# Where the stores of attention rows are issued, and how the first expert slot's weights are spread over the steps

## The chip, the cores and the metric

The kernel runs on one core of a Trainium2 chip. The core has five engines that each run their own list of instructions in order: TensorE (PE in the profile; its weight loads are shown apart as PEld), VectorE (DVE), ScalarE (ACT), GpSimd (POOL) and SyncE (SP), which here computes nothing and mainly issues DMAs. ScalarE and GpSimd issue DMAs too; such an issue stands in the profile as ACTq, SPq or POOLq. Instructions of different engines wait for each other through semaphores.

The metric is the device time of one execution in microseconds, given as the median of several runs. "About 1%" below means what a measurement of this kernel can tell from no change.

## The reference

Two stages follow each other. The first is banded attention, 8 batches of 8 heads, 576 positions, 64 values a head; heads 0 to 3 see the last 32 positions, heads 4 to 7 every fourth of the last 128. The second takes the 4608 rows of 512 that come out, picks one of 8 experts for each by a gate, and runs that expert's two layers.

```python
def _attn_ref(q, k, v):                      # 8, 8, 576, 64
    window, dilation = 32, 4
    scores = scale * np.matmul(q, k.transpose(0, 1, 3, 2))
    rel = pos[:, None] - pos[None, :]
    mask_plain = (rel >= 0) & (rel < window)
    mask_dil = (rel >= 0) & (rel < window * dilation) & (rel % dilation == 0)
    ...
    return np.matmul(softmax(scores), v)
...
def _moe_ref(x, modality_id, w_gate, modality_bias, w1, w2):   # x 4608 x 512
    logits = x @ w_gate + modality_bias[modality_id]
    e_idx = np.argmax(logits, axis=1)
    ...
    for e in range(E):                       # w1[e] 512 x 1024, w2[e] 1024 x 512
        mask = e_idx == e
        h = np.maximum(x[mask] @ w1[e], 0.0)
        out[mask] = gate_w[mask, None] * (h @ w2[e])
```

## The kernel before

**Attention steps.** The queries of a batch are cut into 9 units (m = 0 to 8; m below 5 belongs to heads 0 to 3, the rest to heads 4 to 7), 72 units in all, and two units make one step. The main loop runs over the steps t; the code's `state['t']` counts units, so it is 2t. A step computes the scores of its own two units (tile pss), the exponential of the step before (sm), the transposed probabilities (ptt, pT) and the product with the values (po, vw), and for the units of two steps back it divides by the sum: VectorE writes x_sb (L399), a tile with three buffers, each of which holds the rows of two units.

**Stores and loads.** At the end of a step, `Unit.keep(queue)` stores the x_sb of units two steps back to x_dram, two arrays in main memory, one for each half of the heads. Units 1 and 3 of a batch store 256 KB in one DMA (L419), units 6 and 8 store 256 KB (L422), and unit 4 stores 64 KB (L412) and two pieces of 32 KB (L415). Here `keep` is called with ScalarE's queue (L1240), but the two pieces of L415 name SyncE themselves. All loads of attention are in SyncE's list: keys (`load_one`, L118 and L121, tile st), queries (the same lines), values (`load_v`, L141, tile vw), one to three steps ahead of use. Within a step the order is: queries, values, then at the end of the step keys.

**Experts.** The rows are routed into slots of 256 rows of one expert. Four slots hold rows of batches 0 to 2 alone and are made ready during the attention. For a slot, GpSimd gathers its rows by number from x_dram (L313, tile xr); SyncE writes them to x_slot in main memory (L807) and reads them back in another order as xg in four quarters (L813); VectorE transposes them (L958, tile xt, in two halves), ScalarE rounds them to xh (L964), and VectorE subtracts to get the rest, xl (L967). The weights come by `fetch_weights`: each half of w1 in four quarters of 256 KB (L828, tiles w1q), and w2 in four pieces of 512 KB (L831, tiles w2q); ScalarE and VectorE split them in high and low parts, and TensorE multiplies each pair of parts (L1028 for the first layer, L1008 for the second). The first expert matmuls run beside the last attention steps.

**What sets the order.** PE, VectorE, ScalarE and SyncE run in the order in which the program writes their instructions ("manual schedule"). GpSimd's order is set by the scheduler. Background work of the expert stage (routing, gathers, weights) is written as generators, which `advance()` steps at fixed places of each step, one `yield` at a time. `first_slot` (L887) is the one for slot 0: it calls `load_more(0, 1)`, which takes the next piece from `fetch_weights`, at units 48, 62, 64, 66, 67 and 68, and between them steps `prepare_x(0, ...)`, which holds the transposes and xl. One piece there is either 512 KB of w2 or a whole half of w1, that is four DMAs at once. `loads_of[n][1]` counts the pieces of slot n that are out, six being all; `hold` and `ahead` go by it later.

The DMAs that SyncE and ScalarE issue share eight semaphores, which the program gives out in turn.

Of the kernel before, what the change touches and what calls it, by code (L numbers as in the profile page):

```python
# [22 lines left out]
B, H, S, D = 8, 8, 576, 64  # L23
# [35 lines left out]
def kernel(  # L59
# [12 lines left out]
    nc = tc.nc  # L72
# [51 lines left out]
    def load_qk(b, kd, queue=nc.sync):  # L124
        kn = load_one(b, kd, k)
        return load_one(b, kd, q, queue), kn
# [24 lines left out]
    state = {('qk', 0, 0): load_qk(0, 0, nc.scalar)}  # L151
# [45 lines left out]
    KC, FC = DM // P, FF // P  # L197
# [168 lines left out]
    class Unit:  # L366
# [41 lines left out]
        def keep(self, queue):  # L408

            b, xs = self.b, self.xs  # L410
            if self.m == 4:
                queue.dma_start(out=x_dram[0][b * S + TQ * (NTILE - 1):(b + 1) * S, :], in_=xs[0:TQ, 0])  # L412
                rows = x_dram[1][b * S:(b + 1) * S, :].rearrange("(a p) c -> p a c", a=2)[TQ * HT:HP]
                for hp in range(2):
                    nc.sync.dma_start(out=rows[:, :, 2 * D * hp:2 * D * (hp + 1)],  # L415
                                    in_=xs[TQ + HR * hp:TQ + HR * (hp + 1), 0].rearrange("p (a c) -> p a c", a=2))
            elif self.m in (1, 3):
                r0 = b * S + 2 * TQ * (self.m - 1)
                queue.dma_start(out=x_dram[0][r0:r0 + 2 * P, :].rearrange("(u p) c -> p u c", p=P), in_=xs)  # L419
            elif self.m in (6, 8):  # L420
                rows = x_dram[1][b * S:(b + 1) * S, :].rearrange("(a p) c -> p a c", a=2)
                queue.dma_start(out=rows[P * self.ip:P * (self.ip + 1)], in_=xs)  # L422
# [394 lines left out]
    def fetch_weights(si, first):  # L817

        e = nc.sync.value_load(si[0:1, 0:1], min_val=0, max_val=NE - 1)
        kw = {}  # L820
        if not first:
            kw = dict(cond=nc.sync.value_load(si[0:1, 2:3], min_val=0, max_val=1), cond_hint=False)
        w1v = w1[ds(e, 1)].rearrange("o (r m p) f -> (o r) p m f", r=KC, p=BLK)

        def half(i):
            cols = slice(HALFF * P * i, HALFF * P * (i + 1))
            for r in range(KC):
                nc.sync.dma_start(out=w1q[i][BLK * r:BLK * (r + 1)], in_=w1v[r, :, :, cols], **kw)  # L828

        def pair(c):  # L830
            nc.sync.dma_start(out=w2q[c], in_=w2[ds(e, 1), 2 * P * c:2 * P * (c + 1), :].rearrange("o (a p) m -> p (o a) m", p=P), **kw)  # L831

        for piece, i in ((pair, 0), (half, 0), (pair, 1), (pair, 2), (half, 1), (pair, 3)):
            piece(i)
            yield


# [6 lines left out]
    ids_of, si_of, fetching, loads_of = {}, {}, [], {}  # L844
# [22 lines left out]
    def load_more(n, pieces):  # L867

        if n not in loads_of and n in si_of:
            loads_of[n] = [fetch_weights(si_of[n], n == 0), 0]  # L870
        if n in loads_of:
            for _ in range(min(pieces, 6 - loads_of[n][1])):
                next(loads_of[n][0], None)
                loads_of[n][1] += 1
# [12 lines left out]
    def first_slot():  # L887

        prep = prepare_x(0, ids_of[0])
        for n, at in enumerate((48, 62, 64, 66, 67, 68)):  # L890
            while state['t'] < at:
                if n > 2:
                    next(prep, None)
                yield
            load_more(0, 1)
            yield
        yield from prep

# [48 lines left out]
    def prepare_x(n, ids):  # L947


        nu = ids[1]  # L950
        while ('xg', n) not in state:
            yield
        xg = state['xg', n]
        xh = xpre.tile([P, KC, SLOT], F32R, name="xh")
        xl = xpre.tile([P, KC, SLOT], F32R, name="xl")
        for u in range(nu):
            xt = xpre.tile([P, KC, P], F32, name="xt", bufs=1)
            nc.vector.transpose(out=xt.rearrange("p m (g i) -> p g m i", i=BLK),  # L958
                                in_=xg[:, KC * u:KC * (u + 1)].rearrange("p g (m c) -> p g m c", c=BLK))
            if u == nu - 1:  # L960
                taken.add(n)
            yield
            ts = slice(P * u, P * (u + 1))
            nc.scalar.copy(out=xh[:, :, ts], in_=xt)  # L964
            if n == 0:
                yield
            nc.vector.tensor_tensor(out=xl[:, :, ts], in0=xt, in1=xh[:, :, ts].bitcast(F32), op=ALU.subtract)  # L967
            if u < nu - 1:
                yield
        state['x', n] = xh, xl  # L970
# [158 lines left out]
    pairs, queue, late = [], [], []  # L1129
# [26 lines left out]
    for t in range(NPAIR + 4):  # L1156
        state['t'] = 2 * t
        here = [divmod(i, 9) for i in (2 * t, 2 * t + 1)] if t < NPAIR else []
        for b, m in here:
            if m == 0:  # L1160
                state['lT', b] = gwk.tile([2 * LGP, S], F32, name="lT")
            units.append(Unit(b, m, [state['v', b, 0], state['v', b, 1]] if m >= 4 else [state['v', b, 0]], state['lT', b]))
        if here:
            pairs.append(Pair(units[-2:]))
            pairs[t].scores()
            if t < 2:
                keep_busy((4, 8)[t])
        if t == NPAIR - 1:
            sctx.close()
            psum['y'] = ctx.enter_context(tc.tile_pool(name="ps_y", bufs=2, space=PSUM))  # L1170
            assert 'go' in state
            moe = slots(NS, ids_of, ahead, hold)
        if t == 0:
            pieces = qk_chunks(1, *state['qk', 0, 1])
        for b, m in here:
            if b + 1 < B and m in (4, 8):
                kd = 0 if m == 4 else 1
                pieces = pieces + qk_chunks(kd, *state['qk', b + 1, kd])
        step()
        step()  # L1180
        if 0 <= t - 1 < NPAIR:
            pairs[t - 1].exp()
        po = ps_o.tile([P, 2, 512], F32, name="po") if t < NPAIR + 3 else None
        if 0 <= t - 2 < NPAIR:
            pairs[t - 2].attend(po)
        load_next(t, here, q)
        for b, m in here:
            if m in (3, 8) and b + 1 < B:
                state['v', b + 1, m // 8] = load_v(b + 1, m // 8)
        advance()  # L1190
        step()
        step()
        for i, one in enumerate(late):
            one.logits(po[:, i % 2], LG0 if i < 2 else 0)
        for job in po_work:
            job.pop()(po)
        po_work.clear()
        step()
        step()
        if here:  # L1200
            pairs[t].top()
        if 0 <= t - 2 < NPAIR:
            pairs[t - 2].normalize()
            for unit in pairs[t - 2].units:
                queue += unit.turned()
        n = NCHUNK[here[0][1]] if here and t > 1 else (0, 0)
        if t == 1:
            six(pieces, [None, None, po[:, 0], po[:, 1]] + banks(ps_s, "pss"))
            pieces = []
        chunks(n[0], True)  # L1210
        for one in late:
            one.gather_logits()
            if one.last:
                tasks.append((one.b, background(one.b)))
        for b, m in here:
            if m < 8:
                shift_v(b, m // 4, (0, 1, 2, 3, 3, 0, 1, 2)[m])
        late = []
        advance()
        step()  # L1220
        step()
        if 0 <= t - 1 < NPAIR:
            pairs[t - 1].probsT()
        advance()
        step()
        step()
        if t - 2 == NPAIR - 1:
            late, queue = queue, []
            store(late[:2])
            if late[2:]:  # L1230
                store(late[2:], awk.tile([P, 8, KW], F32, name="sm").rearrange("p j w -> p (j w)"))
        elif queue:
            late, queue = queue[:2], queue[2:]
            store(late)
        chunks(n[1], False)
        step()
        step()
        if 0 <= t - 2 < NPAIR:
            for unit in pairs[t - 2].units:
                unit.keep(nc.scalar)  # L1240
        load_next(t, here, k)
        advance([*round_of, B - 1] if moe and here else range(-1, B))
        if t == NPAIR + 2:
            octx.close()
            psum['h'] = ctx.enter_context(tc.tile_pool(name="ps_h", bufs=2, space=PSUM))
            psum['o'] = ctx.enter_context(tc.tile_pool(name="ps_o1", bufs=1, space=PSUM))
            break
# [42 lines left out]
```

## Time and profile before

| | |
|---|---|
| runs, median of 3 | 696.42 us (694.96, 702.29, 696.42) |
| the profiled execution | 702.78 us, of which its span is 701.1 us |
| granted TensorE clock over the span, mean | 0.973 |
| PE busy | 647.6 us, 92% |
| PE weight loads (PEld) | 565.6 us, 81% |
| VectorE busy | 481.5 us, 69% |
| ScalarE busy | 385.5 us, 55% |
| GpSimd busy | 260.6 us, 37% |
| DMA | 99.12 MB, mean 141 GB/s |
| stores of 256 KB, x_dram<-x_sb, from ScalarE | 32 |
| 256 KB quarters of w1, from SyncE | 152 |

The profile is of one execution, and this one took 6.4 us more than the median of the runs. "busy" is time in which an engine ran instructions; register, semaphore and DMA-issuing instructions are not counted. A row of the timeline reads: start in us from the span's start, duration, engine, line of the program, operation, tile written <- tiles read, form; in brackets the idle time ahead of it and what ended that. A row of waits reads: who waits, at which line, what it waited for, then total us, number of waits and the longest one.

### The profile page before, as it was taken

The numbers are of one execution on the slowest core, as the hardware profiler recorded it, in microseconds if no ns is written. First come the engines' busy times: TensorE is split into PE (matmuls) and PEld (weight loads), VectorE is DVE, ScalarE is ACT, GpSimd is POOL, SyncE is SP. The second block draws the span as 40 slices with busy tenths as digits, with TensorE's granted clock in tenths as the row PEclk, the third lists the DMA queues.
The fourth block names the chain that finished last, engine by engine and source line by source line (L and its number), as shares of the span: only waits on it lengthen the run. The fifth ranks groups of instructions, "written<-read, shape, count | busy, mean of one in ns | idle before, by whom it ended". The sixth has DMA issues, their size and how long they took to land. (4 is left out here: it accounts for less than half of the span.)

```text
span 701.1 us, 17716 instructions
## 1 busy us (share of the span) xinstructions
PE 647.6 (92%) x6461; PEld 565.6 (81%) x6462; DVE 481.5 (69%) x1074; ACT 385.5 (55%) x754; POOL 260.6 (37%) x315
## 2 busy tenths in 40 slices
PE   6899899799885889987999999999999999999994
PEld 3788787688774678776999999989999999999983
DVE  4788678568664777845666776677666766677662
ACT  1666655546533554544665566556665566556652
POOL 8333545535644474745233331333133322311110
PEclk9999999989998899997999999999999999999997
DMA  9968858848799743747223325933223325931550
GB/s 188 211 172 205 198 133 189 194 115 205 156 191 223 185 78 104 136 126 216 83 89 93 121 76 135 271 123 104 78 76 105 121 74 136 266 112 57 141 157 13
DMA packets 131679, 99.12 MB, mean 141 GB/s; under 512 B 67761, under 2 KB 111795, under 8 KB 131589
## 3 DMA queue, kind: packets, MB, share of 16 engines
q1 hardware_dynamic: 111156, 69.19, 40.9%
q0 software_dynamic: 8048, 19.20, 9.5%
q10 hardware_dynamic: 12384, 9.57, 4.5%
q8 instruction: 52, 0.85, 0.6%
q14 instruction: 39, 0.31, 0.2%
HBM read 127.52 MB, written 29.39 MB: 224 GB/s over the span
## 5 line engine op out<-in xcount | busy, mean ns | idle before, releaser
L977 DVE TENSOR_TENSOR w2l<-w2q,w2h 128x512 fp32r<-128x512 f32 x152 | 104.8, 690 | 42.3 <-ACT w2h L976 32.5
L1008 PE MATMUL py<-w2h,hh 128*128 128x512 f32 x296 | 119.0, 402 | 0.0
L313 POOL DMA_INDIRECT xr<-x_dram,idt x74 | 82.8, 1118 | 96.1 <-DMA x_slot<-xr 56.7
L1008 PE MATMUL py<-w2h,hl 128*128 128x512 f32 x296 | 117.1, 396 | 0.0
L1008 PE MATMUL py<-w2l,hh 128*128 128x512 f32 x296 | 115.7, 391 | 0.0
L313 POOL DMA_INDIRECT out_dram<-ys,idt x37 | 41.5, 1121 | 199.4 <-ACT ys L1011 124.0
L977 DVE TENSOR_TENSOR w1l<-w1q,w1h 128x512 fp32r<-128x512 f32 x152 | 103.9, 684 | 11.7 <-DMA w2q<-in_moe_w_dram 9.1
L976 ACT CAST w1h<-w1q 128x512 fp32r<-128x512 f32 x152 | 94.6, 622 | 12.6 <-DMA w1q<-in_moe_w_dram 12.6
L1028 PE MATMUL pt<-xh,w1h 128*128 128x256 f32 (+1 forms) x320 | 91.1, 285 | 7.0 <-issue 7.0
L976 ACT CAST w2h<-w2q 128x512 fp32r<-128x512 f32 x152 | 93.1, 612 | 0.6 <-DVE hl L1035 0.5
L1028 PE MATMUL pt<-xh,w1l 128*128 128x256 f32 (+1 forms) x320 | 90.9, 284 | 0.3 <-DVE w1l L977 0.2
L1028 PE MATMUL pt<-xl,w1h 128*128 128x256 f32 (+1 forms) x320 | 90.5, 283 | 0.0
L1028 PE MATMUL ph<-xh,w1l 128*128 128x256 f32 (+1 forms) x288 | 81.0, 281 | 1.6 <-DVE w1l L977 1.6
L1028 PE MATMUL ph<-xl,w1h 128*128 128x256 f32 (+1 forms) x288 | 80.9, 281 | 0.0
L1028 PE MATMUL ph<-xh,w1h 128*128 128x256 f32 (+1 forms) x288 | 80.8, 281 | 0.0
L313 POOL TENSOR_TENSOR sm<-sm,nmx 128x768 f32<-128x768 f32 x36 | 53.0, 1472 | 73.7 <-DVE den L469 61.1
L1034 ACT ACTIVATE hh<-pt 128x256 fp32r<-128x256 f32 (+1 forms) x80 | 30.3, 379 | 82.4 <-PE pt L1028 74.2
L1034 ACT ACTIVATE hh<-ph 128x256 fp32r<-128x256 f32 (+1 forms) x72 | 27.2, 378 | 80.2 <-PE ph L1028 79.3
L1028 PEld LDWEIGHTS pt<-xh,w1h 128*128 128x128 f32 x320 | 61.0, 191 | 11.0 <-issue 7.4
L1008 PEld LDWEIGHTS py<-w2l,hh 128*128 128x128 f32 x296 | 55.9, 189 | 13.9
L464 PE MATMUL po<-vw,pT 96*64 96x65 f32 (+1 forms) x1216 | 58.2, 228 | 8.3 <-issue 6.4
L1028 PEld LDWEIGHTS pt<-xl,w1h 128*128 128x128 f32 x320 | 61.0, 191 | 3.0
(197 smaller groups left out, 1307.7 us busy)
## 6 DMA issues: line engine op xcount, KB each, us to landing
w2q<-in_moe_w_dram SPq DMA_DIRECT2D x76, 512.0 KB
w1q<-in_moe_w_dram SPq DMA_DIRECT2D x152, 256.0 KB
x_slot<-xr SPq DMA_DIRECT2D x18, 512.0 KB
xg<-x_slot SPq DMA_DIRECT2D x72, 128.0 KB
x_dram<-x_sb ACTq DMA_DIRECT2D x32, 256.0 KB
st<-in_k_dram SPq DMA_DIRECT2D x32, 144.0 KB
vw<-in_v_dram SPq DMA_DIRECT2D x16, 288.0 KB
st<-in_k_dram SPq DMA_DIRECT2D x8, 576.0 KB
```

The lines of the kernel that those rows point to most:

```text
L313: ins = tc.keep_in_program_order(getattr(nc.gpsimd, name)(*args, **kw))
L464: nc.tensor.matmul(out=self.pov[r0:r0 + nr, v, g, cs], lhsT=self.pT[:, v, 2 * g + a, r0:r0 + nr], rhs=unit.vts[kd][:, blk, cs], start=True ...
L976: nc.scalar.copy(out=hi, in_=raw)
L977: nc.vector.tensor_tensor(out=lo, in0=raw, in1=hi.bitcast(F32), op=ALU.subtract)
L1008: nc.tensor.matmul(out=py[u], lhsT=ht[:, us], rhs=wt, start=(f + n == 0), stop=(f + n == FC + 1))
L1028: nc.tensor.matmul(out=ph, lhsT=wt[:, c, :], rhs=xt[:, c, 0:cols], start=(c + i == 0), stop=(c + i == KC + 1))
L1034: nc.scalar.activation(out=hh, in_=ph, func=AF.Relu)
```

## The change

It has two parts. First, `keep` is called with SyncE's queue instead of ScalarE's, and the two pieces of L415 take the queue that they are given. All stores of attention rows thus stand in SyncE's list, at the end of a step and ahead of the keys that the same place loads. Second, `fetch_weights` gives the first slot's w1 one quarter at a time, so that this slot's weights come in twelve pieces instead of six. `first_slot` asks for them at units 46, 50, 52, 54, 56, 60, 62, 64, 65, 66, 67 and 68, eleven steps, and steps `prepare_x` after unit 63; the count in `loads_of` is set such that it comes to six with the twelfth.

```diff
@@ keep @@
                 for hp in range(2):
-                    nc.sync.dma_start(out=rows[:, :, 2 * D * hp:2 * D * (hp + 1)],
+                    queue.dma_start(out=rows[:, :, 2 * D * hp:2 * D * (hp + 1)],
                                     in_=xs[TQ + HR * hp:TQ + HR * (hp + 1), 0].rearrange("p (a c) -> p a c", a=2))
@@ fetch_weights @@
             for r in range(KC):
                 nc.sync.dma_start(out=w1q[i][BLK * r:BLK * (r + 1)], in_=w1v[r, :, :, cols], **kw)
+                if first and r < KC - 1:
+                    yield
 
         def pair(c):
             nc.sync.dma_start(out=w2q[c], in_=w2[ds(e, 1), 2 * P * c:2 * P * (c + 1), :].rearrange("o (a p) m -> p (o a) m", p=P), **kw)
+            yield from ()
 
         for piece, i in ((pair, 0), (half, 0), (pair, 1), (pair, 2), (half, 1), (pair, 3)):
-            piece(i)
+            yield from piece(i)
             yield
@@ first_slot @@
-        for n, at in enumerate((48, 62, 64, 66, 67, 68)):
+        for n, at in enumerate((46, 50, 52, 54, 56, 60, 62, 64, 65, 66, 67, 68)):
             while state['t'] < at:
-                if n > 2:
+                if state['t'] > 63:
                     next(prep, None)
                 yield
             load_more(0, 1)
+            loads_of[0][1] = max(n - 5, 1)
             yield
@@ main loop, end of a step @@
             for unit in pairs[t - 2].units:
-                unit.keep(nc.scalar)
+                unit.keep(nc.sync)
         load_next(t, here, k)
```

The line numbers behind the first edit grow by three or four: L958 becomes L962, L967 becomes L971, L831 becomes L833, L1028 becomes L1032.

How the lists move is seen at three places. In the rows below a name such as `x_dram_88<-x_sb` is the array or tile written and the one read, then the shape, and `x2` a row that repeats; `ISA` is a register instruction that goes with a load whose address is computed. SyncE's list around slot 0's rows, before:

```order
L807 DMA x_slot<-xr 128x2x512
L828 ISA
L828 DMA w1q_243<-in_moe_w_dram 32x4x512
L828 ISA
L828 DMA w1q_243<-in_moe_w_dram 32x4x512
L828 ISA
L828 DMA w1q_243<-in_moe_w_dram 32x4x512
L828 ISA
L828 DMA w1q_243<-in_moe_w_dram 32x4x512
L415 DMA x_dram_88<-x_sb 32x2x128 x2
L813 DMA xg<-x_slot 32x8x128 x4
```

The same place of SyncE's list after the change:

```order
L807 DMA x_slot<-xr 128x2x512
L833 ISA
L833 DMA w2q_247<-in_moe_w_dram 128x2x512
L412 DMA x_dram_87<-x_sb 64x256
L415 DMA x_dram_88<-x_sb 32x2x128 x2
L813 DMA xg<-x_slot 32x8x128 x4
L828 ISA
L828 DMA w1q_244<-in_moe_w_dram 32x4x512
L422 DMA x_dram_88<-x_sb 128x2x256
```

Between the write of x_slot and the read of xg there stood four quarters of w1, and now stands one piece of w2, with the store of L412 beside the two of L415. The quarters of the other half of w1 and the store L422 come behind.

SyncE's list over the steps t = 24 to 26 before, with the queries of a batch (L121), its values (L141) and the keys (L118):

```order
L121 DMA st<-in_q_dram 96x4x384
L141 DMA vw_108<-in_v_dram 64x4x128 x2
L141 DMA vw_108<-in_v_dram 16x4x128
L141 DMA vw_108<-in_v_dram 48x4x128
L141 DMA vw_108<-in_v_dram 64x4x128
L141 DMA vw_108<-in_v_dram 32x4x128
L415 DMA x_dram_88<-x_sb 32x2x128 x2
L118 DMA st<-in_k_dram 96x6x64 x4
```

And after the change:

```order
L422 DMA x_dram_88<-x_sb 128x2x256
L121 DMA st<-in_q_dram 96x4x384
L828 ISA
L828 DMA w1q_243<-in_moe_w_dram 32x4x512
L419 DMA x_dram_87<-x_sb 128x2x256
L141 DMA vw_108<-in_v_dram 64x4x128 x2
L141 DMA vw_108<-in_v_dram 16x4x128
L141 DMA vw_108<-in_v_dram 48x4x128
L141 DMA vw_108<-in_v_dram 64x4x128
L141 DMA vw_108<-in_v_dram 32x4x128
L828 ISA
L828 DMA w1q_243<-in_moe_w_dram 32x4x512
```

The stores L422 and L419 have come in from ScalarE's list, and a quarter of w1 stands in each step. Right behind the last row come another store L419, the store L412, the two L415 and the keys.

VectorE's list at slot 0's second transpose, before:

```order
L149 COPY vw_107<-vw_107 32x520
L958 STREAM_TRANSPOSE xt<-xg 128x4x4x32
L609 TENSOR_TENSOR t_3948<-po,eoff 96x48
L967 TENSOR_TENSOR xl<-xt,xh 128x4x128
L438 TENSOR_TENSOR sm<-pss,masks 128x768
```

And after:

```order
L962 STREAM_TRANSPOSE xt<-xg 128x4x4x32
L438 TENSOR_TENSOR sm<-pss,masks 128x768
L444 TENSOR_REDUCE nmx<-sm 128x8
L469 TENSOR_SCALAR den<-po 128x8
L470 RECIPROCAL den<-den 128x8
L399 TENSOR_TENSOR x_sb<-po,den 128x2x2x64 x2
L521 TENSOR_TENSOR lT<-po,lT 64x128 x2
L149 COPY vw_107<-vw_107 32x520 x2
L538 TENSOR_REDUCE dstf<-t_3949 96x6
L624 CAST dst<-dstf 96x6
L625 RECIPROCAL pay<-sume 96x6
L971 TENSOR_TENSOR xl<-xt,xh 128x4x128
```

The add of L609 now stands ahead of the transpose (it is the row before the first one shown), and xl has moved behind the softmax, the normalization and the shift of values (L149) of one step. TensorE's list is the same before and after. ScalarE's list loses the forty stores. In GpSimd's list one gather of slot 2 has moved ahead of a subtract (sm) and one behind an add (t).

## Prediction

> **What bounds the kernel now.** I read the totals first, then the table of windows, to see which stage loses time; then the waits of that stage, and the timeline around the longest wait; last SyncE's own queue. The first fence has the span from the page, then windows in us: start and end, length, busy time of PE, its weight loads, VectorE, ScalarE and GpSimd (instructions in brackets), granted clock, DMA share, GB/s.
>
> ```profile
> span 701.1 us, 17716 instructions
> 140.00:180.00 40.00, 39.03 (x653) 33.09 (x652) 31.46 (x98) 20.88 (x36) 17.89 (x24) 0.91 0.70 166
> 180.00:220.00 40.00, 34.81 (x580) 28.86 (x578) 25.36 (x67) 21.19 (x39) 24.47 (x29) 0.96 0.82 184
> 220.00:245.00 25.00, 15.86 (x244) 12.83 (x241) 13.82 (x34) 8.40 (x14) 8.69 (x12) 0.80 0.76 194
> 340.00:690.00 350.00, 349.48 (x2246) 316.63 (x2245) 247.05 (x435) 211.39 (x438) 90.17 (x82) 1.00 0.41 120
> ```
>
> Half of the span, the experts from 340 us on, is TensorE without a gap (349.48 of 350 us at clock 1.00). Nothing this change touches can shorten that part; it can only start earlier. The attention steps before 245 us are not full: in the last 25 us PE is busy 15.86 us and its clock falls to 0.80. That is where the loads of the first slot's weights now stand. The waits from 20 to 245 us, by VectorE and TensorE (total, times, longest), and the place itself:
>
> ```profile
> DVE xt L958 <- DMA xg<-x_slot: 7.7, 1, 7.7
> DVE x_sb L399 <- DMA x_dram<-x_sb: 1.3, 1, 1.3
> PE po L505 <- ACT ux L482: 7.5, 1, 7.5
> PE po L464 <- issue: 6.4, 15, 1.1
> PE pss L351 <- DMA st<-in_q_dram: 4.1, 4, 1.4
> ...
> 218.59 1.01 DVE L149 COPY vw<-vw 32x520 f32<-32x520 f32 x2
> 227.27 0.71 DVE L958 STREAM_TRANSPOSE xt<-xg 128x512 f32<-128x512 f32 x1 [7.67 <-DMA xg<-x_slot]
> 228.01 0.62 ACT L964 CAST xh<-xt 128x512 fp32r<-128x512 f32 x1 [8.54 <-DVE xt L958]
> 229.29 1.07 PE L505 MATMUL po<-ux,wgs 128*32 128x128 f32 x8 [7.54 <-ACT ux L482]
> ```
>
> One wait stops three engines: VectorE stands 7.67 us at the transpose of slot 0's rows, since xg has not landed; ScalarE's cast waits for it, ux is behind the cast, and TensorE waits 7.54 us for ux. All three work in order, so this is on the path whole. SyncE's list says why xg is late:
>
> ```profile
> 210.44 0.39 SPq L807 DMA_DIRECT2D x_slot<-xr  x1
> 211.04 2.25 SPq L828 DMA_DIRECT2D w1q<-in_moe_w_dram  x4
> 213.39 0.85 SPq L415 DMA_DIRECT2D x_dram<-x_sb  x2
> 214.50 0.51 SPq L813 DMA_DIRECT2D xg<-x_slot  x1
> 219.88 1.29 SPq L813 DMA_DIRECT2D xg<-x_slot  x3
> ...
> 239.09 0.38 SPq L807 DMA_DIRECT2D x_slot<-xr  x1
> 242.89 1.81 SPq L813 DMA_DIRECT2D xg<-x_slot  x4
> ```
>
> Behind x_slot go four quarters of w1q, 1 MB, then one quarter of xg at 214.50; the other three only from 219.88. The DMAs of SyncE and ScalarE take eight semaphores in turn, each waiting until the DMA eight places back has landed; for the second quarter that is ScalarE's 64 KB store of L412, in the engines' queues beside that 1 MB. Slot 1, without w1q in between, shows the chain undisturbed: 3.80 us from x_slot to the first quarter, and all four out in 1.81 us.
>
> **Part by part.** *First slot's weights.* Removed between x_slot and xg: 1 MB of w1q. Added there: one w2q piece of 0.5 MB, and one more store, of 64 KB. By slot 1's rows the quarters would be out at 210.44 + 3.80 + 1.81 = 216.1 instead of 219.88 + 1.29 = 221.2, 5.1 us earlier. The 0.5 MB less ahead of them is another 2.7 us at 194 GB/s. VectorE is free for xg at 218.59 + 1.01 = 219.6. So the wait falls by at least 5.1 us if the traffic brings nothing, and by 7.67 at most; I take the middle, **-6.4 us**.
>
> The PE rows at that place run at half clock. The same groups ran one slice earlier like this, and after the wait like this:
>
> ```profile
> 201.99 0.63 PE L505 MATMUL po<-ux,wgs 128*32 128x128 f32 x8
> 203.60 1.04 PE L454 MATMUL ptt<-ident,sm 128*96 128x128 f32 x8
> 230.87 1.92 PE L454 MATMUL ptt<-ident,sm 128*96 128x128 f32 x8
> ```
>
> L505 takes 1.07 us for 0.63, L454 1.92 for 1.04: 1.3 us together, which goes if PE no longer stands 7.5 us. Bounds 0 (what is left of the wait still lowers the clock) and -1.3; I take **-1.3**.
>
> Moved forward into the steps from about 166 to 213 us: the 1 MB of w1q, and 0.5 MB of w2q by two steps. 1.5 MB at 184 GB/s is 8.5 us of the DMA engines, whose share there is 0.70 to 0.82: over 47 us some 11 us are free. If the pieces fall into the free time it costs nothing; if all loads of the last batch move back by them, up to +8.5. One 256 KB piece per step, with keys and queries loaded one to three steps ahead of use, is nearer the lower end: **+1.5**.
>
> *Stores of rows.* Forty DMAs leave ScalarE's list and stand in SyncE's, at the end of a step ahead of its keys. What ScalarE gains:
>
> ```profile
> 204.73 1.01 ACT L456 COPY pT<-ptt 96x1024 f32<-96x1024 f32 x1
> 205.24 0.36 ACTq L419 DMA_DIRECT2D x_dram<-x_sb  x1
> 205.64 0.58 ACT L482 COPY ux<-pt 128x512 f32<-128x512 f32 x1
> ```
>
> The 0.36 us issue lies under the copy that is still running, so it costs nothing now, and nothing is gained; bounds 0 and -0.36 a store, -14 us if all were bare. On SyncE the forty issues cost 14 us over the stage, covered as long as it waits anyway for work of the same step. What it waits for now, 20 to 245 us:
>
> ```profile
> SPq L141 <- DMA x_dram<-x_sb: 13.4, 6, 3.8
> SPq L141 <- PE po L464: 11.3, 6, 5.8
> SPq L118 <- DMA x_dram<-x_sb: 10.6, 4, 5.7
> SPq L118 <- PE pt L351: 10.2, 2, 5.2
> SPq L415 <- DMA x_dram<-x_sb: 3.7, 1, 3.7
> ```
>
> In 27.7 us of SyncE's time a load stands until a store has landed that ScalarE issues only when it gets to it. On SyncE a store goes as soon as VectorE has normalized, and loads follow sooner. How much reaches the path: TensorE waits 4.1 us for queries. Bounds 0 and -4.1; half, **-2.0**. Queued behind a waiting store are the step's keys, then the next step's queries and values; keys have the most slack.
>
> The Trainium skill, "DMA: Bandwidth & Descriptors", section "Queues, rings and completion order", says that each DMA engine takes turns between the queue rows that have work. By that a store loses its own turn on SyncE's row and lands later, behind the loads; no row here prices it, and it would make this term a loss, the third rival below.
>
> *VectorE and GpSimd.* The second transpose moves behind one small add, and its xl by most of a step. It is the same work on the same engine, with two subtracts of 0.7 us at worst before the first expert matmul: 0, bounds 0 and +0.7. One gather goes ahead of a subtract of 1.47 us, for which GpSimd stood idle 4.93 us and which hides the gather's issue:
>
> ```profile
> 248.16 1.47 POOL L313 TENSOR_TENSOR sm<-sm,nmx 128x768 f32<-128x768 f32 x1 [4.93 <-DVE den L469]
> ```
>
> **Sum.** -6.4 - 1.3 + 1.5 - 2.0 = -8.2 us. The profiled execution took 702.78 us (its span 701.1): 694.6. That execution is 6.4 us above the median of the runs, 696.42; I take the same difference there: **688.2 us**. What is late next is the clock and the DMA latency of the attention steps, not a single wait.
>
> **Rivals.** *xg stays late.* The w2q piece and the stores ahead of it do what w1q did, and the extra 1.5 MB slows the steps before. For it: the DMA share of 0.82 in 180:220. Against it: half the bytes. With -2.6 for the wait, nothing for the clock, -1 for queries and +3 for traffic: 696.42 - 0.6 = 695.8 us.
>
> *The stores were worth more.* With 27.7 us of waits gone, the loads spread out and TensorE's 6.4 us of gaps labelled "issue" inside L464, which lie in times of full DMA engines, shrink too. Then -7.7 - 1.3 - 4.1 - 4 and no traffic cost: 679.3 us. Against it: no row ties those gaps to the stores.
>
> *Slower: stores too late for their buffer.* x_sb has three buffers, and VectorE writes one again two steps after its store. Steps last 6.37 us, from the first and last of 31 exponentials:
>
> ```profile
> 22.53 0.84 ACT L448 ACTIVATE sm<-sm 128x768 f32<-128x768 f32 x1
> ...
> 213.67 0.86 ACT L448 ACTIVATE sm<-sm 128x768 f32<-128x768 f32 x1
> ...
> 172.09 11.11 SPq L141 DMA_DIRECT2D vw<-in_v_dram  x6
> ```
>
> So a store has 12.7 us from normalization to landing. Now this fails once, by 1.3 us. In the new list a store stands behind each group of six value loads, and the group at 172.09 held SyncE for 11.11 us. If that stays so, a store starts when its time is nearly over, and VectorE, then TensorE, wait. There are some 14 groups of value loads behind which a store stands; the loss passes the gain of 8.2 at 0.6 us for each, and at 1.2 us the time is 696.42 - 8.2 + 17 = 705 us. Against it: most of the 11 us was a wait for ScalarE's store, which is now ahead in the same list. By the rule on turns above, it would be this rival.
>
> **How the numbers follow.** Forecast (684 to 693 us) 0.52; xg stays late (693 to 700) 0.20; stores worth more (below 684) 0.13; slower by the buffer (above 700) 0.15. The time is the forecast's, 688.2. The range 682 to 699 leaves out about 0.07 below and 0.13 above. About 1% is what a measurement of this kernel can tell from no change: 689.5 and 703.4. Faster: 0.13 and 0.33 of the forecast, 0.46. Within 1%: the other 0.19, the first rival's 0.20 and 0.02 of the last, 0.41. Slower: 0.13.
>
> **What would show it.** Right: VectorE's wait for xg under 3 us, the four xg issues within 2.5 us, PE's clock in the slice of the wait above 0.9, no row of SyncE waiting more than 8 us in all for x_dram, and the first expert matmul some 8 us earlier than now. Wrong: a wait of L399 for x_dram of more than 3 us in total (third rival), more than 6 us of PE waiting for queries (traffic), or an unchanged wait for xg. If the experts start earlier and the end doesn't move, the stage from 245 to 340 us has taken it back.

## The result and the profile after

The changed kernel took 690.35 us, the median of 20 runs (684.57 to 699.33), and the kernel before 699.06 us, the median of 20 (693.83 to 705.35). The ratio is 0.9887, with a 95% interval of 0.9858 to 0.9917: 7.9 us less of 699.06 (the two medians as they stand are 8.7 us apart). The forecast was 688.2 us and 8.2 us less. The profiled execution took 694.29 us, 3.9 us above its median; the one before had lain 3.7 us above the median of the 20 runs, 6.4 above that of the first three.

The span of the changed kernel, and its table of windows (start and end, length, busy time of PE, its weight loads, VectorE, ScalarE and GpSimd, granted clock, DMA share, GB/s):

```profile
span 692.3 us, 17695 instructions
140.00:180.00 40.00, 35.16 (x638) 30.02 (x635) 30.79 (x94) 21.27 (x38) 21.47 (x28) 0.96 0.83 173
180.00:220.00 40.00, 31.87 (x522) 26.81 (x521) 22.89 (x62) 19.44 (x35) 18.41 (x23) 0.87 0.95 226
220.00:245.00 25.00, 22.55 (x275) 18.77 (x274) 19.28 (x49) 12.61 (x21) 16.32 (x18) 0.87 0.47 128
340.00:690.00 350.00, 341.83 (x2189) 308.73 (x2188) 240.22 (x423) 205.86 (x426) 89.44 (x81) 1.00 0.41 118
```

The DMA share in 180:220 rose from 0.82 to 0.95 and the clock there fell from 0.96 to 0.87: the 25 us that had been thin are better filled, and the 40 us ahead of them are worse. Part of that is only a shift: the windows are fixed in time, and the step that reads xg, which lay in 220:245 before, now lies in 180:220. In the same way 341.83 us in the last row is no gap; this kernel's last matmul starts at 682.23 us, the other's at 691.21. Its waits from 20 to 245 us (who, at which line, for what; total, times, longest):

```profile
DVE x_sb L399 <- DMA x_dram<-x_sb: 13.8, 7, 6.1
PE pss L351 <- DMA st<-in_k_dram: 3.9, 1, 3.9
DVE xt L962 <- DMA xg<-x_slot: 3.1, 1, 3.1
PE po L505 <- ACT ux L482: 2.7, 1, 2.7
PE pss L351 <- DMA st<-in_q_dram: 1.6, 2, 1.4
```

VectorE's wait for xg is 3.1 us instead of 7.67, which looks like the forecast come true. The new first line does not: VectorE now waits 13.8 us for its row buffers. The longest of these waits stands just ahead of the step that reads xg, in VectorE's timeline:

```profile
194.05 0.96 DVE L438 TENSOR_TENSOR sm<-pss,masks 128x768 f32<-128x768 f32 x1
204.28 0.42 DVE L399 TENSOR_TENSOR x_sb<-po,den 128x256 f32<-128x256 f32 x1 [6.10 <-DMA x_dram<-x_sb]
209.20 0.96 DVE L438 TENSOR_TENSOR sm<-pss,masks 128x768 f32<-128x768 f32 x1 [2.71 <-PE pss L436]
```

The subtract of the masks opens a step on VectorE, so this step took 209.20 - 194.05 = 15.15 us, where the mean was 6.37. A late VectorE has little to wait for at xg, which was on its way meanwhile. So the 3.1 us alone say nothing for the weights.

Last, how much of the gain is there when the experts start: the group of first-layer matmuls of the kernel before and of the changed one (shortest, median and longest in ns, then first and last start in us):

```profile
L1028 PE MATMUL pt<-xh,w1h x320: 221/282/579, 242.0 to 686.9; 128*128 128x256 f32 x152, 128*128 128x128 f32 x8
```

```profile
L1032 PE MATMUL pt<-xh,w1h x320: 221/282/582, 230.3 to 677.9; 128*128 128x256 f32 x152, 128*128 128x128 f32 x8
```

From the first expert matmul to the end of the span there were 701.1 - 242.0 = 459.1 us before and 692.3 - 230.3 = 462.0 after. The end moves with that start; the stage behind it gave back 2.9 us in this pair of profiles. Over all fourteen profiles of this record that stretch is 457.1 to 464.9 us long, while its start lies anywhere from 216.3 to 245.5; so most of what the profiles differ by lies ahead of the first expert matmul. Single profiles of one kernel differ more than the change is worth, as the next section shows, so sizes are read from the ratios and only mechanisms from the profiles.

### The profile page after: what moved, and what is told of

It reads as the page before. It is cut to its first block, busy times and chain, and to the rows that moved or that the text cites. A ratio compares the mean times of both kernels' runs of the same rounds, so it can differ in the third digit from the quotient of the medians.

```text
span 692.3 us, 17695 instructions
## 1 busy us (share of the span) xinstructions
PE 648.2 (94%) x6462; PEld 566.8 (82%) x6462; DVE 483.4 (70%) x1074; ACT 384.5 (56%) x754; POOL 259.5 (37%) x315
## 5 line engine op out<-in xcount | busy, mean ns | idle before, releaser
L313 POOL DMA_INDIRECT xr<-x_dram,idt x74 | 81.4, 1100 | 94.3 <-DMA x_slot<-xr 44.3
L981 DVE TENSOR_TENSOR w1l<-w1q,w1h 128x512 fp32r<-128x512 f32 x152 | 103.8, 684 | 12.5 <-ACT w1h L980 12.5
L1032 PE MATMUL pt<-xh,w1h 128*128 128x256 f32 (+1 forms) x320 | 91.4, 286 | 6.7 <-ACT w1h L980 6.7
L1032 PE MATMUL pt<-xh,w1l 128*128 128x256 f32 (+1 forms) x320 | 91.4, 286 | 1.0 <-DVE w1l L981 1.0
L1032 PE MATMUL pt<-xl,w1h 128*128 128x256 f32 (+1 forms) x320 | 90.7, 283 | 0.0
L1032 PE MATMUL ph<-xh,w1l 128*128 128x256 f32 (+1 forms) x288 | 81.1, 282 | 1.7 <-DVE w1l L981 1.6
L1032 PE MATMUL ph<-xl,w1h 128*128 128x256 f32 (+1 forms) x288 | 80.9, 281 | 0.0
L1032 PE MATMUL ph<-xh,w1h 128*128 128x256 f32 (+1 forms) x288 | 80.8, 281 | 0.0
L1032 PEld LDWEIGHTS pt<-xh,w1h 128*128 128x128 f32 x320 | 61.3, 192 | 11.0 <-ACT w1h L980 7.3
L1032 PEld LDWEIGHTS pt<-xl,w1h 128*128 128x128 f32 x320 | 61.3, 192 | 3.1
L1032 PEld LDWEIGHTS pt<-xh,w1l 128*128 128x128 f32 x320 | 61.5, 192 | 2.0 <-DVE w1l L981 2.0
```

Of the source, the lines that this page charges most:

```text
L313: ins = tc.keep_in_program_order(getattr(nc.gpsimd, name)(*args, **kw))
L981: nc.vector.tensor_tensor(out=lo, in0=raw, in1=hi.bitcast(F32), op=ALU.subtract)
L1032: nc.tensor.matmul(out=ph, lhsT=wt[:, c, :], rhs=xt[:, c, 0:cols], start=(c + i == 0), stop=(c + i == KC + 1))
```

## The experiments

The kernels of one call ran on one chip together with runs of the kernel before. Its median there was 705.07 us in the first call (stores alone, weights alone, six buffers, pieces behind xg), 697.71 in the second (the changed kernel and the kernel before again, keys ahead, GpSimd) and 705.96 in the third (the rest). Only ratios are compared.

**The two parts, each alone, twice.** Stores alone: the kernel before with

```diff
-                    nc.sync.dma_start(out=rows[:, :, 2 * D * hp:2 * D * (hp + 1)],
+                    queue.dma_start(out=rows[:, :, 2 * D * hp:2 * D * (hp + 1)],
...
-                unit.keep(nc.scalar)
+                unit.keep(nc.sync)
```

> The kernel before with all stores of rows in SyncE's list, the weights as before. A, the stores carry the change: the gaps of TensorE at L464 labelled issue (6.4 us before) fall under 1.5 us, the steps up to unit 46 gain about 9 us, the wait for xg stays at 5 us or more, and the ratio to before is 0.985 to 0.991 (about 690 us). B, the split as the prediction had it, stores 2.0 us: ratio 0.995 to 0.999, gaps at L464 above 4 us.

> The stores alone once more, beside the weights alone on one chip. A, the parts help each other: 0.992 to 0.997 here, so that stores and weights alone multiply to above 0.995 where the whole change has 0.988. B, the stores are all of it: 0.985 to 0.990.

Measured: 0.9946 (0.9907 to 0.9985), and again 0.9867 (0.9793 to 0.9941). Weights alone: the changed kernel with those two lines as before.

> The changed weights' twelve pieces, with the stores on ScalarE's queue as before. A, the stores carry the change: the wait for xg falls by 3 us or more, but a step near unit 62 gets longer by the weights' traffic, gaps at L464 stay above 4 us, ratio 0.996 to 1.003. B, the split as the prediction had it, weights 6.2 us: ratio 0.988 to 0.994.

> The weights alone once more. A, without the stores' move they bring nothing: 0.998 to 1.006, the wait for xg 5 us or more, and SyncE's loads wait 15 us or more for stores that ScalarE issues. B, the first measurement was off: 0.988 to 0.995, the wait for xg under 4 us.

Measured: 1.0039 (1.0002 to 1.0075) and 0.9999 (0.9958 to 1.0041). So the weights' twelve pieces bring nothing by themselves, twice, and the stores bring between 0.5 and 1.3%; the two intervals of the stores overlap, and neither of them decides between the two ranges expected. The gaps labelled issue at L464, which the expectation tied to the stores, did not follow it: 5.0 and 2.9 us with the stores alone, 5.7 and 2.8 with the weights alone, 0.2 in the changed kernel, and none in the second profile of the kernel before. They are not an effect of the change.

Of the weights alone (second run), the waits of 20 to 245 us:

```profile
PE po L505 <- ACT ux L482: 8.0, 1, 8.0
DVE xt L962 <- DMA xg<-x_slot: 7.9, 1, 7.9
PE pss L351 <- DMA st<-in_q_dram: 6.6, 3, 3.1
SPq L141 <- DMA x_dram<-x_sb: 23.2, 6, 7.0
SPq L118 <- DMA x_dram<-x_sb: 14.0, 5, 4.8
```

And of the stores alone (second run):

```profile
DVE xt L958 <- DMA xg<-x_slot: 2.7, 1, 2.7
PE po L505 <- ACT ux L482: 2.2, 1, 2.2
PE pss L351 <- DMA st<-in_q_dram: 0.3, 1, 0.3
SPq L419 <- DVE lT L514: 22.2, 3, 8.9
SPq L419 <- DVE x_sb L399: 16.7, 9, 4.4
```

The wait for xg, which the prediction gave to the weights, goes with the stores, though the 1 MB of w1q still stands between x_slot and xg there. Expectation A of either part's first run had it the other way round, too. In the other pair of runs it was the same: 7.5 us with the weights alone, 2.7 with the stores alone. The timelines say how. Weights alone, SyncE, then two stores of ScalarE, then VectorE:

```profile
203.78 13.31 SPq L141 DMA_DIRECT2D vw<-in_v_dram  x6
217.28 0.38 SPq L807 DMA_DIRECT2D x_slot<-xr  x1
...
202.27 0.37 ACTq L419 DMA_DIRECT2D x_dram<-x_sb  x1
207.26 0.36 ACTq L419 DMA_DIRECT2D x_dram<-x_sb  x1
...
227.58 0.71 DVE L962 STREAM_TRANSPOSE xt<-xg 128x512 f32<-128x512 f32 x1 [7.89 <-DMA xg<-x_slot]
```

Stores alone, SyncE and VectorE:

```profile
194.11 7.72 SPq L419 DMA_DIRECT2D x_dram<-x_sb  x2
201.92 5.51 SPq L141 DMA_DIRECT2D vw<-in_v_dram  x6
207.62 0.38 SPq L807 DMA_DIRECT2D x_slot<-xr  x1
...
220.16 0.71 DVE L958 STREAM_TRANSPOSE xt<-xg 128x512 f32<-128x512 f32 x1 [2.66 <-DMA xg<-x_slot]
```

The six value loads ahead of x_slot hold SyncE 13.31 us in one and 5.51 in the other, where the two stores ahead of them hold it another 7.72. In the first, 9.0 of the time from 200 to 218 us are two waits of these loads until a store of ScalarE has landed: 7.0 for the store of 202.27 (the second load goes out at 211.43) and 2.0 for that of 207.26, which is issued in the middle of them. So they wait for landings, 8 to 9 us after the issue, and ScalarE's late issue is at most the smaller part. In the second, SyncE waits at the stores instead, until VectorE has written the rows (the two SPq rows above).

That is so over the whole stretch from 20 to 245 us. The rows of SyncE's loads that wait for stores add up to 25.0 and 41.3 us in the two profiles of the kernel before and are gone with the stores alone, but the rows of the stores' own waits come to 67.1 and 63.1 us there; all of SyncE's rows together are 101.0 and 118.8 us before and 95.5 and 97.9 with the stores alone. SyncE is not so much freed as held at another place.

VectorE is free for xg at 227.58 - 7.89 = 219.7 and at 220.16 - 2.66 = 217.5. So two numbers decide the wait: the lead, from x_slot's issue to VectorE being free, and the chain, from x_slot's issue to the transpose. Worked out in the same way for the profiles of all these kernels, in us:

| kernel | lead | chain | wait for xg |
|---|---|---|---|
| before, two profiles | 9.2 and 5.0 | 16.8 and 14.1 | 7.7 and 9.1 |
| weights alone | 4.5 and 2.4 | 12.0 and 10.3 | 7.5 and 7.9 |
| stores alone | 9.8 and 9.9 | 12.5 and 12.5 | 2.7 and 2.7 |
| both, the change | 7.5 and 4.7 | 10.5 and 12.2 | 3.1 and 7.5 |

Alone, the weights' new places shorten the chain by some 4 us in the mean and the lead by about as much, so the wait stays. The stores' move shortens the chain by 3 and lengthens the lead by nearly 3: counted from the subtract that opens VectorE's step, x_slot goes out 2.1 us earlier in the mean and VectorE comes 0.7 later. The weights on top of it take 3.8 us from the lead and 1.1 from the chain. For both parts together the wait is 5.3 us in the mean, 8.4 before.

**The changed kernel and the kernel before again.**

> The changed kernel once more, on the same chip as the kernels beside it. A, the two parts help each other (alone they were 0.995 and 1.004): ratio 0.984 to 0.992, and the long step at 194 to 209 us of the first profile was chance and is under 9 us here. B, the parts add up: ratio 0.996 to 1.001.

> The kernel before, profiled on the same chip as the others, for the steps. A, SyncE's waits for stores that ScalarE issues are there again, 20 to 35 us in all, and the wait for xg is 5 us or more. B, they were chance: under 10 us, and the wait for xg under 3 us.

Measured: 0.9877 (0.9836 to 0.9918) for the changed kernel, so the first result holds. Its waits in this profile:

```profile
DVE xt L962 <- DMA xg<-x_slot: 7.5, 1, 7.5
PE po L505 <- ACT ux L482: 7.4, 1, 7.4
DVE x_sb L399 <- DMA x_dram<-x_sb: 5.0, 4, 2.3
PE pss L351 <- DMA st<-in_q_dram: 3.7, 3, 3.1
SPq L807 <- DMA w2q<-in_moe_w_dram: 2.1, 1, 2.1
```

And those of the kernel before:

```profile
DVE xt L958 <- DMA xg<-x_slot: 9.1, 1, 9.1
PE po L505 <- ACT ux L482: 9.0, 1, 9.0
PE pss L351 <- DMA st<-in_q_dram: 7.4, 5, 3.3
SPq L141 <- DMA x_dram<-x_sb: 16.9, 5, 5.4
SPq L118 <- DMA x_dram<-x_sb: 16.3, 6, 5.5
```

The step of 15 us is gone (6.84 here; the one that begins at 178.28 now takes 10.67), and with it the short wait for xg: it is 7.5 us, with the kernel faster all the same. The last row of the first fence shows one way in which the weights take back what they give: x_slot itself stands 2.1 us until a piece of w2 has landed. The kernel before has SyncE's waits for stores again, over 33 us at values and keys in these two rows. This profile was its fastest run of the call (691.39 us), so the two spans, 687.4 and 689.6, are not a measure of the change.

**Six buffers for the rows.** The changed kernel with x_sb alternately from its own three buffers and from three that the high parts of w1 use later:

```diff
-                self.xs = state['xs'] = awk.tile([P, 2, 4 * D], F32, name="x_sb", bufs=3)
+                if state['nx'] % 2 == 0 and self.b < B - 1:
+                    self.xs = wsp.tile([P, KC, P], F32R, name="w1h")...
+                else:
+                    self.xs = awk.tile([P, 2, 4 * D], F32, name="x_sb", bufs=3)
```

> The changed kernel with three more buffers for x_sb (they lie in the high parts of w1, which are idle until the experts start). A, the 13.8 us that VectorE waits at L399 for stores are on the path in the step at 194 to 209 us: the wait falls under 2 us, that step from 15.4 us to 10 or less, ratio to before 0.980 to 0.986 (about 686 us). B, TensorE's wait for keys and queries in the same step lasts as long: the L399 wait goes, TensorE's wait for st grows or stays at 5 us, ratio 0.987 to 0.991 as the changed kernel.

The tiles alternate in all batches but the last. Measured: 0.9869 (0.9822 to 0.9917), not clearly lower than the changed kernel's 0.9887 and 0.9877; the interval holds B's range and part of A's. In its one profile, of the longest of its seven runs, VectorE waits for no store at L399, as the edit meant. What those waits cost the changed kernel isn't settled; the interval leaves up to some 5 us.

**Seven pieces behind xg.**

```diff
-            load_more(0, 1)
+            for _ in range((1, 1, 1, 1, 1, 0, 0, 0, 2, 2, 2, 1)[n]):
+                load_more(0, 1)
```

> The changed kernel with the last seven of the twelve pieces (2.5 MB) issued behind xg, at units 66 and 68 in place of 60 to 68. A, the moved weights make the long step at 194 to 209 us: it falls from 15.4 us to 11 or less, the wait for xg under 2 us, ratio to before 0.980 to 0.986. B, the attention's own loads and stores make it: the step stays above 13 us, ratio 0.987 to 0.991. C, the pieces now come too late for the experts: TensorE waits more than 3 us longer for weights behind 230 us.

Measured: 0.9912 (0.9867 to 0.9958). Expectation A's range is out; B's lies inside the interval. C is not seen: in its one profile, of the longest of its twelve runs, TensorE's waits for parts of the experts' weights from 230 to 340 us are 6.1 us, and 8.5 in the first profile of the changed kernel. Without any weights between x_slot and xg the kernel is no faster.

**Keys ahead of the stores.** `load_next(t, here, k)` moved above the stores at the end of the step.

> The changed kernel with each step's keys loaded ahead of the stores in SyncE's list. A, the keys behind the waiting stores cost something (TensorE waited 3.9 us for keys at 201 us): ratio 0.003 to 0.008 below that of the changed kernel beside it. B, the keys have slack and the stores are the more urgent, so that VectorE waits longer at L399 (over 20 us instead of 13.8): ratio as high or higher by up to 0.008.

Measured: 0.988 (0.9843 to 0.9917) beside 0.9877 for the changed kernel: no difference. TensorE's wait for queries was 0.8 us, and 3.7 in the changed kernel beside it; VectorE's at L399 was 10.5 and 5.0, and not the 20 of expectation B. One wait went and the other grew, and that keys stand behind the stores costs nothing that these runs can tell.

**All stores on GpSimd's queue.** The changed kernel with `unit.keep(nc.gpsimd)`; then the same with the weights' six pieces as before; then with slot 0's rows earlier:

```diff
-first_rows(0, (t0 + 12, t0 + 13, t0 + 16, t0 + 17, t0 + 18, t0 + 20, t0 + 22))
+first_rows(0, (t0 + 10, t0 + 11, t0 + 12, t0 + 13, t0 + 14, t0 + 18, t0 + 20))
```

> The changed kernel with all stores of rows on GpSimd's queue. A, what counts is that SyncE's loads no longer wait for stores that another engine issues: SyncE has no wait for x_dram<-x_sb at loads, the wait for xg is under 4 us, ratio 0.982 to 0.992 as the changed kernel or better. B, it counts that the stores stand in SyncE's own list: ratio above 0.995. C, GpSimd has no room for forty issues (1.0 to 1.1 us each, 40 us): VectorE or ScalarE wait for its subtract (sm) 10 us more, ratio above 1.00.

> The kernel before with all stores of rows on GpSimd's queue and the weights' six pieces as before. A, the stores carry it also here and the weights' pieces add little: 0.975 to 0.983, within 0.006 of the 0.977 with the twelve pieces. B, the twelve pieces need SyncE free of stores and then bring what the prediction gave them (6.2 us): 0.984 to 0.990.

> The stores on GpSimd's queue and the twelve pieces, and slot 0's rows gathered two to five units earlier, their write to x_slot and read as xg two units earlier. A, the wait for xg is a matter of the gather's start alone: it falls from 4.9 to under 1 us, TensorE's wait at L505 too, ratio 0.967 to 0.974. B, the earlier traffic takes it back in the steps before: the wait falls, ratio 0.975 to 0.982.

Measured: 0.9771 (0.9723 to 0.9819), 0.9793 (0.9727 to 0.9858) and 0.9733 (0.9663 to 0.9803). The first lies below the changed kernel beside it, 0.9877 (0.9836 to 0.9918), with no overlap: 678.54 us against 689.58. With the six old pieces it is no worse than the runs can tell, though the interval of 0.9793 also reaches into the range of expectation B. The first one's totals and waits:

```profile
PE 639.9 (95%) x6461; PEld 560.7 (83%) x6462; DVE 492.3 (73%) x1074; ACT 384.5 (57%) x754; POOL 299.9 (44%) x371
```

```profile
DVE xt L962 <- DMA xg<-x_slot: 4.9, 1, 4.9
PE po L505 <- ACT ux L482: 4.8, 1, 4.8
PE pss L351 <- DMA st<-in_q_dram: 0.8, 1, 0.8
DVE x_sb L399 <- DMA x_dram<-x_sb: 0.3, 1, 0.3
```

GpSimd is busy 299.9 us instead of 259.5 in the changed kernel, and still only 44% of the span (an issue of 256 KB took 0.78 us, where the expectation had 1.0 to 1.1); SyncE waits for no store, VectorE for none but 0.3 us, TensorE 0.8 us for queries. The wait for xg, at 4.9 us, is longer than expectation A had it. With the rows gathered earlier the transpose has no wait at all:

```profile
215.59 0.71 DVE L962 STREAM_TRANSPOSE xt<-xg 128x512 f32<-128x512 f32 x1
```

Yet the ratio is not clearly lower than the other two, and its interval holds A's range and most of B's. What it gains to remove the wait that the prediction was built on is not settled: 0.004 and 0.006 lower, with intervals of 0.005 to 0.007 to either side. What exactly gives GpSimd's queue its advantage over SyncE's (a list of its own, so that nothing queues behind a waiting store, or a path of its own to the DMA engines) was not taken apart.

## Why the total came right and the split did not

The sum of -8.2 us met a measured -7.9, and the time lay in the forecast's own range. That is luck: two terms were wrong, and their errors cancel. The sum was made of -6.2 for the weights and -2.0 for the stores, and the runs give the weights alone 1.0039 and 0.9999, about nothing, and the stores alone 0.9946 and 0.9867, -3.8 and -9.3 us of 700. Whether the weights add anything on top of the stores isn't settled: 0.9887 and 0.9877 for both lie between the two measurements of the stores, and 0.9771 and 0.9793 on GpSimd's queue, with the twelve pieces and with six, do not differ by what the runs can tell.

*xg, -6.4.* This is the step that failed. The prediction shortened SyncE's list between x_slot and xg and kept x_slot and VectorE at their old times. Both moved: x_slot now comes behind pieces of weights for which it waits, and VectorE is earlier. A chain shorter by 5.1 us at least was nearly right for the weights: alone they take some 4 us from it. But the lead shrank by as much. The row of the second quarter had named a store of ScalarE and the 1 MB, and the credit went to the 1 MB; either one shortens the chain, and only the stores' move lengthens the lead. With the stores alone the wait is 2.7 us twice, with the weights alone 7.5 and 7.9, with both 3.1 and 7.5.

*The clock, -1.3.* Not seen. Adding up, in windows of 5 us from 20 to 245, the length times what the clock lacks of 1 gives 10.2 us for the kernel before and 13.6 for the changed one (8.5 and 11.9 in the second pair). Half-clock stretches moved to other steps instead of going.

*Traffic, +1.5.* No run measures it alone. What the weights do take shows where it was not looked for: in the lead, which they shorten by 2 to 5 us.

*Stores, -2.0, bounds 0 and -4.1.* Mis-sized: the term measured -3.8 and -9.3. The first lies in the bounds, and its interval (-1.1 to -6.5) holds the -2.0; that of the second (-4.1 to -14.5) does not. The 27.7 us of SyncE's waits did go, but the list did not get shorter by them: the stores' own waits took their place. TensorE's wait for queries fell from 4.1 and 7.4 us to 0.4 and 0.3 with the stores alone, all that the bound had allowed. Beyond the bound lay a second effect: x_slot goes out earlier and its chain is shorter, and the wait for xg falls by 5 us or more. The bound was drawn around one consumer of SyncE's list, and the list has several. How much of the gain each of them makes up is not shown; in the second profile of the changed kernel the gain stands beside a wait for xg of 7.5 us.

*ScalarE's forty issues at nothing.* All kernels that gained have them off ScalarE's list, so the runs alone don't exclude that this is the gain. The timelines of the kernel before do, as far as the cost of the issues goes: over 35 of the 40 stores ScalarE's next computing instruction starts before or just as the one ahead ends, and the gaps at the other five sum to 2.5 us in one profile and 1.7 in the other.

*Rivals.* The buffers' rival named its sign, more than 3 us at L399, and the sign came: 13.8 and 5.0 us. Its price did not: six buffers gave no clear gain. A store in SyncE's list does land late when other DMAs are ahead of it: the one that VectorE awaited until 204.28 had been issued at 193.60, right behind keys and queries of 576 KB each. The Trainium skill, "DMA: Bandwidth & Descriptors", section "Queues, rings and completion order", has the engines take turns between rows, by which a store loses its turn in the fuller row; that fits this one store, and the total went the other way. The rival that the stores were worth more was right about them (the chance given was 0.13) and wrong about the issue gaps. The rival that xg stays late happened in the second profile, wait and all, with a gain of 1.2% beside it.

*The signs.* Of those named for right, two came in both profiles of the changed kernel: the four issues of xg took 2.46 and 1.78 us, and no row of SyncE waits more than 2 us for x_dram. The wait for xg (3.1 and 7.5 us) and the clock (0.87 in 180:220 and in 220:245 of the first profile) missed theirs, and the first expert matmul came 11.7 us earlier in the first pair and 3.0 in the second. Of those named for wrong, the waits at L399 came.

## What to carry to other kernels

A wait can be shortened by freeing the list that feeds it as much as by clearing the place just ahead of it: ask when the first DMA of the chain is issued, not only what stands between it and the last. Where a load waits until another engine's store has landed, every load behind it is late; moved into the same list, the store can wait there itself, so add up all waits of the list before and after, and look at each of its consumers. A single profile in which a wait became short proves little while the step before it became long; the same part run alone, twice, decides.

## What the runs showed that was not expected

An issue from GpSimd is dearer than one from SyncE, and the kernel with all 56 stores on it (the forty and the sixteen of L415) was the faster. The Trainium skill, "DMA: Bandwidth & Descriptors", section "Issuing engine by pattern", calls SyncE's and ScalarE's path generally faster; by the clock of one issue these rows agree (shortest, median and longest in ns), 782 ns against a median of 383 at the same line from SyncE in the changed kernel:

```profile
L419 POOL DMA_DIRECT2D x_dram<-x_sb x16: 725/782/937, 26.9 to 229.0; - x16
```

By the kernel's time they do not: 0.9771 against 0.9877. What an issue costs did not decide.

A single wait of 7 us stands behind 245 us, where the prediction did not look; it had named the clock and DMA latency as what is late next, "not a single wait". TensorE needs a high part of w1, which ScalarE casts when w1 has landed. Before (ScalarE, TensorE) and after (TensorE):

```profile
319.15 0.62 ACT L976 CAST w1h<-w1q 128x512 fp32r<-128x512 f32 x1 [9.41 <-DMA w1q<-in_moe_w_dram]
319.82 0.58 PE L1028 MATMUL pt<-xh,w1h 128*128 128x256 f32 x1 [6.99 <-issue]
```

```profile
310.31 0.58 PE L1032 MATMUL pt<-xh,w1h 128*128 128x256 f32 x1 [6.65 <-ACT w1h L980]
```

It is 6.5 to 7.2 us in ten of the fourteen profiles. With the stores alone it is not there in one piece (3.7 and 3.5 us in several, at w1l), and yet the time from the first expert matmul to the end is no shorter, 461.2 and 460.6 us; so what its removal would gain is not shown.

The calls, each on another chip, differ by about as much as the change is worth: the medians of the kernel before were 697.71, 705.07 and 705.96 us. That the chip makes this is not shown. Among the runs of the kernel before in the first call the shorter ones tend to have the higher granted clock, from a span of 698.1 us at 0.973 to one of 708.1 at 0.958, with exceptions (705.3 at 0.972).
